# The last product of three chained layers by Strassen's scheme, and halves of a product of two weight matrices added as they are emptied

## The chip, the cores and the metric

The kernel runs on one core of a Trainium2 chip. The metric is device time in microseconds (us); less is better. The time of the kernel before is 646.93 us, the median of three runs (645.35 to 648.14).

## What is computed

The reference chains attention, a gated feed-forward layer and a second block; only the second block is changed.

```python
# x: 896 tokens x 768, from attention (2 batches of 448 tokens, 12 heads) and the gated layer
def _moe2_ref(x, w1, w2, w3, w_out):
    a = x @ w1                 # 896 x 1024
    b = x @ w2                 # 896 x 1024
    h = a * b @ w3             # 1024 x 1024
    return (h @ w_out)         # 1024 x 768
```

The kernel multiplies the two weight matrices first: M = w3 @ w_out (1024 x 768), while it works on earlier stages, and then needs one last product, out = (a * b) @ M. The inputs of the weights come as 64-bit numbers and are turned into 32-bit ones on the core.

## The kernel before

Everything is held transposed: 128 features on the partitions, tokens along the free axis, in two halves `b` of 448 tokens. Every product is taken in three matmuls (`gemm`, lines 791 to 793): each operand is split into a high and a low part of a shorter float format, and high*high, high*low and low*high are added up in one PSUM bank. A split is a copy into the short format (`half`, lines 180 to 184, on ACT, DVE or POOL) and a subtraction on DVE (`rest`, line 187).

The stages that matter here, in order of time, are made from the list `seq` in `experts`:

- "up" and "down" of the gated layer, first half (`h` = 0);
- "prod": the second half of M's inner dimension, eight row blocks `kb` by two column halves of 384, 12 matmuls of 384 columns each. The first half was taken earlier, between the attention's steps, by `last_product`. Both halves of M are emptied from PSUM by `out_`'s `copy` and written to DRAM by its `store` (line 613) as two separate arrays `m32[0]` and `m32[1]`;
- "up" and "down", second half (`h` = 1);
- "two": the products with w1 and w2, for each of eight feature blocks `f` and both token halves 18 matmuls with each matrix. The first result is copied out of its bank (line 839), the second multiplied by it (line 855), and the product `z` is split (`first`, `second`);
- "out": the last product. For each of six output blocks `d` and both token halves, 24 matmuls of 448 columns (eight inner blocks, three matmuls each). Its weights, blocks of M, come back from DRAM through `weights` with kind "sum": two loads of 256 KB (line 255), one addition on DVE (`sum_`, line 259), then a split. The bank is copied out by ACT and stored (line 939).

The order of the instructions on every engine is not written by hand. `Plan` simulates the five engines with a cost for each step, gives every step a rank, and issues on each engine the ready step of lowest rank; the result is a fixed order in which each engine's queue then runs. A step that waits holds up all that stands behind it on its engine. Buffers are rings with a fixed number of turns: `raw` (3) for loaded weights, `hl` (4) for split weights, `sg` (4) for 448-column scratch, `mo` (2) for M's blocks on their way out, and pairs of PSUM banks `m`, `o`, `s` used in turn. The big buffers `A`, `B` (at that time the split input `ys` of "two", one for each token half), `C` (the split w_out of "prod"), `xr0`, `xr1` and `u` have one turn each. SP issues all loads and stores.

Of the kernel before, what the change touches and what calls it, by code (L numbers as in the profile page):

```python
# [38 lines left out]
HJ = CF2 // 2  # L39
NRAW, NHL, EARLY = 3, 4, 4  # L40
# [125 lines left out]
def body(ctx: ExitStack, tc, qk, v, cap, wgv, wdn, rg, w12, w3t, wo2, out):  # L166
# [8 lines left out]
    m32 = dram.tile([2, CF2, P, DM], F32, name="m32")  # L175
# [34 lines left out]
    def layer(es, bounded):  # L210
# [6 lines left out]
        rings |= {n: 1 for n in ("A", "B", "C", "xr0", "xr1", "u")}  # L217
# [20 lines left out]
        def weights(kind, src, n, m, rank, when, get, makes, uses, after=(), ready=()):  # L238

# [8 lines left out]
            def load(e):  # L248
                if kind == "f64":
                    st["t"] = t = ring(wst, "raw", [P, n, m, 2], I32, "wraw")  # L250
                    e.dma_start(out=t, in_=src)
                else:
                    st["t"] = t = ring(wst, "raw", [P, 2, n, m], name="wraw")
                    for i in range(2):
                        e.dma_start(out=t[:, i], in_=src[i])

            def sum_(e):
                st["w"] = st["t"][:, 0]
                e.tensor_tensor(st["w"], st["t"][:, 0], st["t"][:, 1], op=ALU.add)
# [31 lines left out]
            if kind == "f64":  # L291
                a = add(unary, high, rank + 0.1, after=[last], uses=[raw])
                c = add(unary, low, rank + 0.2, after=[last], uses=[raw])
                a = add(("DVE", two), join, rank + 0.3, after=[a, c], uses=[raw])
                last = add(("DVE", two), sign, rank + 0.4, after=[a], uses=[raw])
            else:
                last = add(("DVE", two), sum_, rank + 0.1, after=[last], uses=[raw])
# [289 lines left out]
        def prep_wo(q, rank, when, step):  # L587

            done = wo_done[q] = []

            def get_wo(r):
                def get(new):
                    if q not in wo:
                        wo[q] = ring(big, "BC"[q], [P, 2, HJ, DM], F32R, "wo")
                    return wo[q][:, 0, r : r + 1, :], wo[q][:, 1, r : r + 1, :]

                return get

            for r in range(HJ):
                done.append(  # L600
                    list(weights("f64", wo2[q * HJ + r], 1, DM, rank + (10 * step * r if q else r), when + step * r, get_wo(r), [] if r else [wob[q]], [wob[q]] if r else [],
                                 ready=[done[0][0]] if r else []))
                )

        def out_(q, kb, n, get):
            st = {}

            def copy(e):
                st["o"] = ring(tp, "mo", [P, NH])
                half(st["o"], get()[:, :NH], e)  # L610

            def store(e):
                e.dma_start(out=m32[q, kb][:, n * NH : (n + 1) * NH], in_=st["o"])

            return copy, store

        def last_product():
# [13 lines left out]
            for kb in range(CF2):  # L631
                w3b[kb] = buf("hl")
                w3_done[kb] = list(weights("f64", w3t[0, kb], HJ, P, 1000.5 if kb == 0 else 1003 + kb, 0 if kb == 0 else 3 + kb * 3.5, get_w3(kb), [w3b[kb]], []))

# [14 lines left out]
            for kb in range(CF2):  # L649
                bb = [buf("m") for _ in range(2)]  # L650
                last = {}
                for y in range(2 * HJ):
# [4 lines left out]
                    if r == HJ - 1:  # L657
                        copy, store = out_(0, kb, n, lambda kb=kb, n=n: mb[kb, n])
# [68 lines left out]
        def experts(over, stored):  # L727
# [7 lines left out]
            mv = [m32[q].rearrange("k p c -> p k c") for q in range(2)]  # L735
            seq += [("out", [t[:, i * HJ : (i + 1) * HJ, d * P : (d + 1) * P] for t in mv], HJ, d, i) for d in range(CD) for i in range(2)]
# [13 lines left out]
            def w_of(k):  # L750
                if k not in w_done:
                    what, src, n, _, _ = seq[k]
                    wb[k] = buf("hl")
                    kind, after = ("sum", stored) if what == "out" else ("f64", [])
                    w_done[k] = list(weights(kind, src, n, P, 2000 + 10 * k, 60 + k, get_w(k), [wb[k]], [], after=after))
# [4 lines left out]
            zrb = {b: buf("xr%d" % b) for b in range(B)}  # L760
            u, z, zr, yp, ys, banks, sg = {}, {}, {}, {}, {}, {}, {}
# [6 lines left out]
            n_out = len(seq) - 2 * CD  # L768
            while k < n_out:
                order += [(k, b) for b in range(B)]  # L770
                k += 1
            for d in range(CD):
                order += [(n_out + 2 * d, b) for b in range(B)]
# [4 lines left out]
            def z_at(part, f, b):  # L778
                if f < HF:
                    return u["t"][:, part, f, tok(b)]  # L780
                return zr[b][:, 2 * (f - HF) + part, :]
# [19 lines left out]
            u_done, u_read, y_done, yp_done, y_alloc, yp_alloc, z_done, zr_alloc = {}, {0: [], 1: []}, {}, {}, {}, {}, {}, {}  # L801
            sgb, sg_done = {}, {}
            u_alloc = []
            for s, (k, b) in enumerate(order):
# [6 lines left out]
                half_tiles = [k, k + 1] if what == "out" else [k]  # L811
                a, g = None, 0
                for kk in half_tiles:
                    src, need, held = {
                        "up": (x_at, x_done[b], [xsb[b]]),
                        "down": (u_at, None, [ub]),
                        "prod": (wo_at, None, [wob[1]]),
                        "two": (y_at, y_done.get(b), [yb[b]]),
                        "out": (z_at, None, [ub, zrb[b]]),
                    }[what]  # L820
                    ready = w_of(kk)
                    for c in range(seq[kk][2]):
                        if what == "prod":
                            need = wo_done[1][c]
                        if what == "down":
                            need = u_done[i, b, c]
                        if what == "out":
                            need = z_done[b, g]
                        total = 2 * HJ if what == "out" else n
                        a = add(("PE", 0.53 if what == "prod" else 0.615), gemm(kk, b, c, total, g, src, tag if a is None else None, k), rank + 0.1 * g,  # L830
                                after=[a] + list(need) + ready, makes=[bb] if a is None else [], uses=[wb[kk]] + held + ([bb] if a is not None else []))
                        g += 1
# [17 lines left out]
                elif what in ("up", "two"):  # L850
                    key = (f, b) if what == "up" else ("z", f, b)
                    at = u_at if what == "up" else z_at
# [4 lines left out]
                    def first(e, key=key, f=f, b=b, at=at, what=what):  # L857
                        if what == "up" and "t" not in u:
                            u["t"] = up().tile([P, 2, HF, NT], F32R, tag="u", name="u", bufs=1)
                        if what == "two" and f == HF and b not in zr:  # L860
                            zr[b] = ring(big, "xr%d" % b, [P, 2 * (CF2 - HF), S], F32R, "zr")
                        half(at(0, f, b), sg[key], e)

                    def second(e, key=key, f=f, b=b, at=at):
                        rest(at(1, f, b), sg[key], at(0, f, b), e)
# [3 lines left out]
                    if what == "up":  # L869
                        if not u_alloc:  # L870
                            makes, held, more = [ub], [], list(over)
                        else:
                            more = u_alloc + (u_read[0] if f >= HF else [])
                    elif f >= HF:
                        held = [zrb[b]]
                        if f == HF:
                            makes, held = [zrb[b]], []
                        else:
                            more = zr_alloc[b]
                    else:  # L880
                        more = u_read[0] + u_read[1]
                    i1 = add(("ACT", 0.58), first, late + 0.1, after=[a] + more, makes=makes, uses=[sgb[key]] + held)
                    if what == "up" and not u_alloc:
                        u_alloc.append(i1)
                    if what == "two" and f == HF:
                        zr_alloc[b] = [i1]
                    i2 = add(("DVE", 0.64), second, late + 0.2, after=[i1], uses=[sgb[key], *(makes + held)])
                    if what == "up":
                        u_done[f // HF, b, f % HF] = [i1, i2]
                    else:  # L890
                        z_done[b, f] = [i1, i2]
                elif what == "prod":
                    copy, store = out_(1, f, b, lambda k=k, b=b: banks[k, b])
                    mo = buf("mo")
                    a = add(dict(DVE=0.57, ACT=0.52), copy, late, after=[a], makes=[mo], uses=[bb])
                    stored.append(add(("SP", 0.45), store, -50, after=[a], uses=[mo], size=P * NH * 4))
                elif what == "down":
# [32 lines left out]
                else:  # L930
                    ob = buf("sg")
                    st = {}

                    def copy(e, b=b, k=k, st=st):
                        st["o"] = ring(tp, "sg", [P, S], name="ob")
                        half(st["o"], banks[k, b][:, :S], e)

                    def store(e, d=f, b=b, st=st):
# [74 lines left out]
```

## Time and profile before

| | us |
|---|---|
| median of three runs | 646.93 (645.35 to 648.14) |
| the profiled execution's own time | 644.65 |
| its span, first to last instruction | 642.5 |
| TensorE (PE) busy | 625.0 |
| VectorE (DVE) busy | 390.0 |
| ScalarE (ACT) busy | 277.2 |
| GpSimd (POOL) busy | 162.8 |

The table tells shares of the whole span. What a change in one stage is worth is read from that stage, so the rows below go by stretches of time: "prod" runs from 290.5 to 323.8 us, "two" from 459.7 to 576.7 us, "out" from 576.7 to 636.4 us. Matmuls overlap, so the start of one to the start of the next is the pace, and the duration of one is longer than that.

### The profile page before, as it was taken

Reading aid. Unit: us, or ns where it says so; the run is one execution under the profiler, and the core shown is the slowest. Engines: PE = TensorE matmul, PEld = TensorE weight load, DVE = VectorE, ACT = ScalarE, POOL = GpSimd, SP = SyncE. Lnnn points to the kernel's source line nnn. Section 1 sums busy time; section 2 is a strip of 40 time slices with the busy share of each in tenths; the row PEclk is TensorE's granted clock in tenths of the full one; section 3 lists DMA queues with packets and bytes.
Section 4 is the critical chain, followed back from the end, with each engine's and each line's share of the span. In section 5 each row is a group of like instructions: output and inputs, shape, how many; then the busy total and the mean of one; then the engine's idle time right before and its main releaser. Section 6 shows DMA issues by size and latency. Waiting matters only on the chain.

```text
span 642.5 us, 7766 instructions
## 1 busy us (share of the span) xinstructions
PE 625.0 (97%) x2985; PEld 529.0 (82%) x2985; DVE 390.0 (61%) x474; ACT 277.2 (43%) x383; POOL 162.8 (25%) x161
## 2 busy tenths in 40 slices
PE   6899999999999999999999999999999999999996
PEld 2455556669999999999999999999999999999995
DVE  2898999979867677524765555576565564332300
ACT  6798788965434344223433332233332232121111
POOL 1747532213133344222422222211132221000000
PEclk9899999999999999999999999999999999999999
DMA  8554542325345444225863222333222332224411
GB/s 313 171 201 142 186 142 78 112 73 185 112 153 186 138 141 153 93 71 187 258 211 99 98 99 99 107 129 107 99 99 98 99 118 96 66 65 142 141 46 47
DMA packets 33886, 82.91 MB, mean 129 GB/s; under 512 B 2992, under 2 KB 21040, under 8 KB 33840
## 3 DMA queue, kind: packets, MB, share of 16 engines
q1 hardware_dynamic: 33840, 82.33, 38.4%
q8 instruction: 25, 0.41, 0.3%
q14 instruction: 21, 0.17, 0.1%
HBM read 73.27 MB, written 9.04 MB: 128 GB/s over the span
## 4 chain that ended last, share of the span: by engine, by line
PE 82%; DVE 9%; ACT 5%; issue 2%; POOL 1%; DMA 1%; SPq 0%; ACTq 0%; POOLq 0%; DVEq 0%
PE bank L791 25%; PE bank L793 25%; PE bank L792 25%; PE po L471 3%; DVE sm L499 3%; PE pss L440 2%; ACT t L448 1%; DVE wraw L277 1%; ACT t L454 1%; DVE wraw L281 1%; DVE th L187 1%; PE bank L642 1%; POOL xraw L507 1%; PE bank L644 1%; PE bank L643 1%
## 5 line engine op out<-in xcount | busy, mean ns | idle before, releaser
L273 POOL TENSOR_SCALAR wraw<-wraw 128x768 int32<-128x768 uint32 (+1 forms) x71 | 77.6, 1093 | 195.0 <-DMA wraw<-in_w 85.2
L187 DVE TENSOR_TENSOR whl<-wraw,whl 128x768 fp32r<-128x768 f32 (+1 forms) x80 | 70.1, 876 | 79.5 <-POOL whl L184 65.4
L791 PE MATMUL bank<-xn,whl 128*128 128x448 f32 x288 | 105.6, 367 | 0.5 <-POOL wraw L273 0.5
L792 PE MATMUL bank<-xn,whl 128*128 128x448 f32 x288 | 105.6, 367 | 0.0
L793 PE MATMUL bank<-xn,whl 128*128 128x448 f32 x288 | 105.6, 367 | 0.0
L277 DVE SCALAR_TENSOR_TENSOR wraw<-wraw 128x768 int32<-128x768 int32 (+1 forms) x76 | 70.7, 931 | 48.8 <-POOL wraw L273 43.8
L184 POOL TENSOR_SCALAR whl<-wraw 128x768 fp32r<-128x768 f32 (+1 forms) x47 | 42.4, 902 | 202.0 <-PE bank L793 160.8
L281 DVE SCALAR_TENSOR_TENSOR wraw<-wraw 128x768 int32<-128x768 int32 (+1 forms) x76 | 79.2, 1042 | 1.7
L791 PE MATMUL bank<-u,whl 128*128 128x448 f32 x216 | 79.3, 367 | 0.0
L793 PE MATMUL bank<-u,whl 128*128 128x448 f32 x216 | 79.3, 367 | 0.0
L792 PE MATMUL bank<-u,whl 128*128 128x448 f32 x216 | 79.3, 367 | 0.0
L471 PE MATMUL po<-t,v 128*128 128x448 f32 (+1 forms) x192 | 75.1, 566 | 2.6 <-DVE xraw L182 1.4
L264 ACT ACTIVATE wraw<-wraw 128x768 f32<-128x768 f32 (+1 forms) x59 | 52.1, 882 | 45.8 <-DMA wraw<-in_wgv 16.3
L791 PE MATMUL bank<-y,whl 128*128 128x448 f32 x192 | 70.7, 368 | 0.0
L792 PE MATMUL bank<-y,whl 128*128 128x448 f32 x192 | 70.7, 368 | 0.0
L793 PE MATMUL bank<-y,whl 128*128 128x448 f32 x192 | 70.7, 368 | 0.0
L471 PEld LDWEIGHTS po<-t,v 128*128 128x128 f32 (+1 forms) x192 | 31.5, 192 | 33.5 <-issue 25.4
L791 PEld LDWEIGHTS bank<-xn,whl 128*128 128x128 f32 x288 | 54.1, 188 | 5.7 <-POOL wraw L273 0.8
L793 PEld LDWEIGHTS bank<-xn,whl 128*128 128x128 f32 x288 | 54.1, 188 | 4.9
L792 PEld LDWEIGHTS bank<-xn,whl 128*128 128x128 f32 x288 | 54.1, 188 | 4.7
L180 ACT ACTIVATE whl<-wraw 128x768 fp32r<-128x768 f32 (+1 forms) x33 | 28.3, 858 | 42.2 <-PE bank L793 40.6
L448 ACT ACTIVATE t<-pss,small 128x896 f32<-128x896 f32 x42 | 41.9, 998 | 10.3 <-PE pss L440 8.4
(89 smaller groups left out, 938.8 us busy)
## 6 DMA issues: line engine op xcount, KB each, us to landing
wraw<-in_wgv SPq DMA_DIRECT2D x24, 768.0 KB, 4.4
wraw<-in_w SPq DMA_DIRECT2D x16, 768.0 KB, 4.2
wraw<-in_wdn SPq DMA_DIRECT2D x12, 768.0 KB, 4.2
wraw<-in_w3t SPq DMA_DIRECT2D x16, 512.0 KB, 3.9
wraw<-in_wo SPq DMA_DIRECT2D x8, 768.0 KB, 6.7
m<-mo SPq DMA_DIRECT2D x32, 192.0 KB, 2.7
wraw<-m SPq DMA_DIRECT2D x24, 256.0 KB, 3.2
v<-in_v SPq DMA_DIRECT2D x12, 448.0 KB, 3.8
```

The source lines that it names most:

```text
L180: nc.scalar.activation(out_, in_, AF.Copy)
L184: nc.gpsimd.tensor_scalar(out_, in_, 1.0, 1.0, op0=ALU.mult, op1=ALU.mult)
L187: e.tensor_tensor(lo, raw, r32(hi), op=ALU.subtract)
L264: e.activation(h, h, AF.Copy, scale=2.0**-112)
L273: e.tensor_scalar(l, l.bitcast(U32), 0.876 * 2.0**-29, 0.49, op0=ALU.mult, op1=ALU.add)
L277: e.scalar_tensor_tensor(l, h, 3, l, op0=ALU.logical_shift_left, op1=ALU.bitwise_or)
L281: e.scalar_tensor_tensor(l, h, -(2**31), l, op0=ALU.bitwise_and, op1=ALU.bitwise_or)
L448: e.activation(chunks[g], s[:, :, :S], AF.Tanh, scale=tsc)
L471: e.matmul(pos[2 * p + i][:, :S], vals[p][rows, 6 if c == 3 else 2 * c + i, :], x, start=start, stop=stop)
L791: e.matmul(dst, whi[:, c, :], src(0, g, b), start=(g == 0), stop=False)
L792: e.matmul(dst, whi[:, c, :], src(1, g, b), start=False, stop=False)
L793: e.matmul(dst, wlo[:, c, :], src(0, g, b), start=False, stop=(g == total - 1))
```

## The change

**The last product.** The list `seq` ends with "two"; the stage "out" is replaced by a loop of its own over three pairs `D` of output blocks. M's block pair (two blocks `r` of 128 output features), the inner blocks (even and odd ones) and the token halves make a 2 x 2 by 2 x 2 block product. By Strassen's scheme (Winograd's form) it is taken as seven products for eight; each is four inner blocks `q` by three matmuls of 448 columns. Four sums of blocks of M per `D` (`combine`, S1 to S4) and four differences of blocks of `z` per pair of feature blocks (`less`, the operands 4, 5, 3 and 6) are needed, three more splits of `z` per pair of feature blocks, and additions when the banks are emptied (`plus`): per `D` one copy on ACT and seven additions on DVE for four copies on ACT.

**Homes of z.** The 28 split operands of z lie in `u`, `C`, `xr0`, `xr1` and a new buffer `ux`; a ring `sx` of two holds raw differences.

**Loads of M.** M is stored as one array. Per `D` two loads of 512 KB: the first pair into the ring `raw`, the second and third into `A` and `B`.

**Halves of M.** The first half of M goes to `m32_half`. In "prod" each half block of it (192 KB) is loaded back into an `mo` or `sg` buffer ahead of time, and DVE adds the bank to it on the way out, where DVE or ACT copied the bank before.

The diff, cut to its core:

```diff
-    m32 = dram.tile([2, CF2, P, DM], F32, name="m32")
+    m32 = dram.tile([CF2, P, DM], F32, name="m32")
+    m32_half = dram.tile([CF2, P, DM], F32, name="m32_half")
...
+        rings["sx"] = 2
...
-            mv = [m32[q].rearrange("k p c -> p k c") for q in range(2)]
-            seq += [("out", [t[:, i * HJ : (i + 1) * HJ, d * P : (d + 1) * P] for t in mv], HJ, d, i) for d in range(CD) for i in range(2)]
...
+                    if op == 0:
+                        parts(0, [d], late + 0.1)
+                    elif op == 3:
+                        z_raw[q, 4] = less(4, 3, 0, None, [d, z_raw[q, 0]], late + 0.1)
+                        parts(4, [z_raw[q, 4]], late + 0.2)
+                    elif op == 1:
+                        parts(1, [d], late + 0.1)
+                    else:
+                        t2 = less(5, 2, 4, 4, [d, *z_done[q, 4]], late + 0.1)
+                        parts(5, [t2], late + 0.2)
+                        t3 = less(3, 2, 3, 3, [d, z_raw[q, 4]], late + 0.3)
+                        parts(3, [t3], late + 0.4)
+                        t4 = less(6, 1, 5, 1, [t2, *z_done[q, 1]], late + 0.5)
+                        parts(2, [d], late + 0.6)
+                        parts(6, [t4], late + 0.7)
...
                 elif what == "prod":
-                    copy, store = out_(1, f, b, lambda k=k, b=b: banks[k, b])
-                    mo = buf("mo")
-                    a = add(dict(DVE=0.57, ACT=0.52), copy, late, after=[a], makes=[mo], uses=[bb])
+                    tag = "sg" if (2 * f + b) % 3 else "mo"
+                    load, copy, store = out_(1, f, b, lambda k=k, b=b: banks[k, b], tag)
+                    mo = buf(tag, late)
+                    x = add(("SP", 0.45), load, rank * 0.001 + 60 + k - 1.5, after=halves, makes=[mo], size=P * NH * 4)
+                    a = add(("DVE", 0.57), copy, late, after=[a, x], uses=[mo, bb])
...
+            for D in range(CD // 2):
+                rank, when, late = 6000 + 100 * D, 60 + len(seq) + 2 * D, 900 + 10 * D
+                where = ("raw", "A", "B")[D]
...
+                s1 = combine("S1", "A21", "A22", ALU.add, load, 0)
+                s2 = combine("S2", "S1", "A11", ALU.subtract, [s1], 1)
+                s3 = combine("S3", "A11", "A21", ALU.subtract, [s1], 2)
+                s4 = combine("S4", "A12", "S2", ALU.subtract, [s2], 3)
+                jobs = [("A11", 0, load), ("S1", 4, [s1]), ("A12", 1, load), ("S2", 5, [s2]), ("S3", 3, [s3]), ("S4", 2, [s4]), ("A22", 6, load)]
...
+                for n, (name, op, ready) in enumerate(jobs):
...
+                    i1 = add(dict(POOL=0.75, ACT=0.63), first, i, after=ready, makes=[hb], uses=rawb)
+                    i2 = add(("DVE", 0.7), second, i + 0.5, after=[i1], uses=[hb] + rawb)
...
+                    for q in range(NQ):
+                        a = add(("PE", 0.615), prod(name, op, q, tag), rank + n + 0.1 * q, after=[a] + z_done[q, op] + [i1, i2],
...
+                    if name == "A11":
+                        plus("s1", name, None, [a], late)
+                    elif name == "A12":
+                        done = plus("c11", name, "s1", [a], late), "c11", 0, 0
+                    elif name == "S2":
+                        plus("u2", name, "s1", [a], late + 0.1, at="s1")
+                        plus("u4", "S1", "u2", [ends["S1"]], late + 0.2)
+                    elif name == "S3":
+                        done = plus("c22", name, "u4", [a], late + 0.3), "c22", 1, 1
+                        plus("u3", name, "u2", [a], late + 0.4, at="u2")
+                    elif name == "S4":
+                        done = plus("c12", name, "u4", [a], late + 0.5, at="u4"), "c12", 0, 1
+                    else:
+                        done = plus("c21", name, "u3", [a], late + 0.6, at="u3"), "c21", 1, 0
```

## Rows read from the trace of the kernel before

**Rows 1.** The page: span, and busy time of each engine.
```profile
span 642.5 us, 7766 instructions
PE 625.0 (97%) x2985; PEld 529.0 (82%) x2985; DVE 390.0 (61%) x474; ACT 277.2 (43%) x383; POOL 162.8 (25%) x161
```

**Rows 2.** Waits of PE from 158 us on: total, times, longest.
```profile
PE bank L791 <- POOL wraw L273: 0.5, 1, 0.5
```

**Rows 3.** Busy time by stretch: "prod", second "up"/"down", "two", "out".
```profile
core 0: us, PE busy (x) PEld busy (x) DVE busy (x) ACT busy (x) POOL busy (x), PEclk, DMA share, GB/s
290.80:323.80 33.00, 33.00 (x192) 33.00 (x192) 18.53 (x24) 11.81 (x19) 10.46 (x12) 1.00 0.73 238
323.80:459.70 135.90, 135.90 (x659) 123.46 (x658) 79.90 (x106) 48.29 (x70) 28.34 (x26) 1.00 0.33 113
459.70:576.70 117.00, 117.00 (x567) 106.27 (x567) 58.64 (x74) 31.25 (x48) 19.05 (x18) 1.00 0.29 95
576.70:636.40 59.70, 59.69 (x289) 53.88 (x287) 11.55 (x17) 9.73 (x17) 2.47 (x4) 1.00 0.31 96
```

**Rows 4.** Timeline of "out": first and last matmul, last copy, last store's issue.
```profile
576.71 0.37 PE L791 MATMUL bank<-u,whl 128*128 128x448 f32 x1
...
636.02 0.37 PE L793 MATMUL bank<-zr,whl 128*128 128x448 f32 x1
636.48 0.54 ACT L180 ACTIVATE ob<-bank 128x448 f32<-128x448 f32 x1 [4.41 <-PE bank L793]
637.05 0.33 SPq L939 DMA_DIRECT2D out<-ob  x1
```

**Rows 5.** Timeline of PE: fifteen matmuls in first "up"; begin and end of "prod".
```profile
239.78 0.36 PE L793 MATMUL bank<-xn,whl 128*128 128x448 f32 x1
...
242.82 0.36 PE L793 MATMUL bank<-xn,whl 128*128 128x448 f32 x1
...
290.45 0.34 PE L791 MATMUL bank<-wo,whl 128*128 128x384 f32 x1
...
323.58 0.33 PE L793 MATMUL bank<-wo,whl 128*128 128x384 f32 x1
323.76 0.36 PE L791 MATMUL bank<-xn,whl 128*128 128x448 f32 x1
323.96 0.37 PE L792 MATMUL bank<-xn,whl 128*128 128x448 f32 x1
324.17 0.37 PE L793 MATMUL bank<-xn,whl 128*128 128x448 f32 x1
```

**Rows 6.** Groups by shape on DVE and ACT in "two" and "out": busy, mean ns.
```profile
L855 DVE TENSOR_TENSOR sg<-bank,sg 128x448 f32<-128x448 f32 x15 | 9.4, 624 | 18.5 <-PE bank L793 18.5
L187 DVE TENSOR_TENSOR u<-sg,u 128x448 fp32r<-128x448 f32 x12 | 8.2, 679 | 3.2 <-ACT u L180 3.2
L187 DVE TENSOR_TENSOR zr<-sg,zr 128x448 fp32r<-128x448 f32 x3 | 1.9, 624 | 1.3 <-ACT zr L180 1.3
L180 ACT ACTIVATE zr<-sg 128x448 fp32r<-128x448 f32 x3 | 1.7, 579 | 7.7 <-DVE sg L855 7.7
...
L187 DVE TENSOR_TENSOR whl<-wraw,whl 128x512 fp32r<-128x512 f32 x9 | 6.2, 693 | 17.6 <-ACT whl L180 10.2 <-POOL whl L184 7.3
L259 DVE TENSOR_TENSOR wraw<-wraw 128x512 f32<-128x512 f32 x6 | 4.2, 694 | 12.0 <-DMA wraw<-m 12.0
L180 ACT ACTIVATE whl<-wraw 128x512 fp32r<-128x512 f32 x5 | 3.2, 632 | 10.1 <-PE bank L793 10.1
```

**Rows 7.** Groups by shape over the whole span: further DVE and POOL durations.
```profile
L914 DVE TENSOR_TENSOR yp<-bank,yp 128x448 f32<-128x448 f32 x12 | 7.5, 625 | 12.5 <-PE bank L793 12.5
L182 DVE COPY mo<-bank 128x384 f32<-128x384 f32 x10 | 5.3, 541 | 4.9 <-DMA m<-mo 4.8
L277 DVE SCALAR_TENSOR_TENSOR wraw<-wraw 128x512 int32<-128x512 int32 x16 | 12.1, 756 | 18.6 <-POOL wraw L273 18.6
L184 POOL TENSOR_SCALAR whl<-wraw 128x512 fp32r<-128x512 f32 x22 | 15.9, 724 | 108.5 <-PE bank L793 72.9 <-PE bank L644 16.4 <-issue 14.3
```

**Rows 8.** The page's DMA issues: count, KB each, median us to landing.
```profile
wraw<-in_w3t SPq DMA_DIRECT2D x16, 512.0 KB, 3.9
m<-mo SPq DMA_DIRECT2D x32, 192.0 KB, 2.7
wraw<-m SPq DMA_DIRECT2D x24, 256.0 KB, 3.2
```

**Rows 9.** DMA in "prod", 290.8 to 323.8 us: all, by queue, and stores' landing.
```profile
DMA packets 3021, 7.86 MB, mean 238 GB/s; under 512 B 332, under 2 KB 2104, under 8 KB 3018
q1 hardware_dynamic: 3018, 7.81, 72.9%
m<-mo SPq DMA_DIRECT2D x14, 192.0 KB, 3.4
```

**Rows 10.** Timeline of DVE in "prod": last step of two weight blocks.
```profile
308.67 0.69 DVE L187 TENSOR_TENSOR whl<-wraw,whl 128x512 fp32r<-128x512 f32 x1 [0.54 <-POOL whl L184]
313.19 0.96 DVE L187 TENSOR_TENSOR whl<-wraw,whl 128x768 fp32r<-128x768 f32 x1 [0.77 <-POOL whl L184]
```

**Rows 11.** Waits of SP's queue from 280 us on: total, times, longest.
```profile
SPq L251 <- DVE whl L187: 209.0, 37, 9.4
...
SPq L613 <- ACT mo L180: 12.1, 11, 1.7
SPq L613 <- DVE mo L182: 7.3, 5, 2.6
```

More of the change, by code (lines that the diff above doesn't have):

```diff
@@ L39 @@
 HJ = CF2 // 2
+CS = 7 * CF2 // 2
 NRAW, NHL, EARLY = 3, 4, 4
@@ L248, in load @@
             def load(e):
[L249 to L259, printed above, removed]
+                st["t"] = t = ring(wst, "raw", [P, n, m, 2], I32, "wraw")
+                e.dma_start(out=t, in_=src)
             def high(e):
@@ L753, in w_of @@
                     wb[k] = buf("hl")
-                    kind, after = ("sum", stored) if what == "out" else ("f64", [])
-                    w_done[k] = list(weights(kind, src, n, P, 2000 + 10 * k, 60 + k, get_w(k), [wb[k]], [], after=after))
+                    w_done[k] = list(weights(src, n, P, 2000 + 10 * k, 60 + k, get_w(k), [wb[k]], []))
                 return w_done[k]
@@ L810, in experts @@
                 late = 600 + s
[L811 to L832, printed above, removed]
+                src, need, held = {
+                    "up": (x_at, x_done[b], [xsb[b]]),
+                    "down": (u_at, None, [ub]),
+                    "prod": (wo_at, None, [wob[1]]),
+                    "two": (y_at, y_done.get(b), [yb[b]]),
+                }[what]
+                ready, a = w_of(k), None
+                for c in range(n):
+                    if what == "prod":
+                        need = wo_done[1][c]
+                    if what == "down":
+                        need = u_done[i, b, c]
+                    a = add(("PE", 0.53 if what == "prod" else 0.615), gemm(k, b, c, n, c, src, tag if a is None else None, k), rank + 0.1 * c,
+                            after=[a] + list(need) + ready, makes=[bb] if a is None else [], uses=[wb[k]] + held + ([bb] if a is not None else []))
                 if what == "up" and i == 0:
@@ L880, in experts @@
                     else:
[L881 removed]
+                        more = u_alloc + (u_read[0] if f >= HF else [])
                     i1 = add(("ACT", 0.58), first, late + 0.1, after=[a] + more, makes=makes, uses=[sgb[key]] + held)
[L883 removed]
+                    if not u_alloc:
                         u_alloc.append(i1)
[L885 to L886 removed]
@@ L929, in experts @@
                         y_done[b].append(add(("DVE", 0.64), second, late + 0.2, after=[x], uses=[ypb[b], yb[b]]))
[L930 to L938, printed above, removed]
-                        e.dma_start(out=out[d * P : (d + 1) * P, tok(b)], in_=st["o"])
-                    x = add(("ACT", 0.57), copy, late, after=[a], makes=[ob], uses=[bb])
-                    add(("SP", 0.45), store, -50, after=[x], uses=[ob], size=P * S * 4)
+            mv = m32.rearrange("k p c -> p k c")
```

210 lines of the change are left out of this document (155 added, 55 removed).

## Prediction

> **What bounds the kernel now.** I read the page's busy times first: PE is busy 625.0 of 642.5 us, the next engine 390.0 [rows 1]. A share can hide idle time, so I asked next what PE waits for from 158 us on, when attention is over: one wait of 0.5 us in all [rows 2]. Then the stretches, with the granted clock beside them: in "prod", the second "up"/"down", "two" and "out" PE is busy to the last hundredth, at a granted clock of 1.00, the upper level (2.4 GHz), while DVE has 56%, 59%, 50% and 19% [rows 3]. From 158 us to the end the time is thus the number of matmuls times their pace. A matmul taken out of these stages is worth its pace, as long as nothing else comes late for PE.
>
> The pace is read from starts. "Out" is 288 matmuls (6 blocks x 2 token halves x 24); from the first start to the last are 287 steps in 636.02 - 576.71 = 59.31 us, or 0.2067 us each [rows 4]. This pace is not the only one the trace shows: in the first "up" fifteen matmuls of the same size take 242.82 - 239.78 = 3.04 us, 0.2027 each. The step up comes with the second 448-column matmul after "prod" (324.17 - 323.96 = 0.21) and stays to the end [rows 5]. The granted clock reads 1.00 on both sides [rows 3], so no change of the clock's level explains it. I don't know what sets it; it comes back as a rival.
>
> **The change part by part.** *Matmuls.* 3 pairs `D` x 7 products x 4 inner blocks x 3 = 252 for 288, of the same 448 columns. 36 fewer x 0.2067 = 7.44 us off, all of it on the path. The ends of this price are the two paces, 7.30 and 7.44; I take the one of this stage.
>
> The Trainium skill (TensorE: Matmul & The Clock Gate, Back-to-back issue gap) gives N / 2.4 + 2.5 ns for an isolated gap, an estimate of 189 ns for 448 columns, by which the 36 would give 6.8 us. The trace disagrees at 206.7 ns [rows 4], and the sum goes by the trace.
>
> *The differences and splits of z, in "two".* Per pair of feature blocks 4 subtractions and 3 further splits: on DVE 4 + 3 steps, on ACT 3. A subtraction of two scratch buffers has no row; the nearest reads the same two operands' worth from SBUF at 448 columns, 0.624 to 0.679 us [rows 6], and I take 0.65. Four pairs: 28 x 0.65 = 18.2 us on DVE, 12 x 0.58 = 7.0 on ACT. DVE goes from 58.6 to some 77 of 117 us, ACT from 31.3 to 38 [rows 3]: beside PE's work, and free as long as the last results come in time.
>
> *That end of "two".* It is where the change adds a dependency. Before, "out" began with blocks finished long ago and reached the last one after 21 matmuls, 4.3 us later. Now the fourth product (S2, with operand 5) needs the difference made from the very last bank. The cover is the three products before it, 36 x 0.2067 = 7.44 us. The chain is product out of the bank 0.62, difference 0.65, ACT half 0.58, rest 0.62 [rows 6], with some 0.1 us between steps about 2.9 us: covered, with 4.5 us over. If DVE takes all eight late z steps in an unlucky order, 8 x 0.64 + 0.58 = 5.7 us, still covered. Only if the preparation of the first `D` (4 sums and 7 rests, 11 x 0.69 = 7.6 us) stood ahead as well would it take 13.3 and stall PE for 5.9 us. Those ranks are behind z's, and the weights' buffers are free far earlier, so I take 0 and keep 0 to 5.9 as the bound.
>
> *The sums of M's blocks and their splits.* Per `D` 4 sums, 7 rests and 7 emptying additions on DVE: 4 x 0.694 + 7 x 0.693 + 7 x 0.625 (an addition of a bank to an SBUF buffer, line 914) = 12.0 us [rows 6, 7]. The sums read every second block of 128; no row reads so, the nearest are the contiguous sum, 0.694, and a step that reads every second word, 0.756 [rows 6, 7], which adds 0.2 us at most. One `D` lasts 84 x 0.2067 = 17.4 us on PE, so DVE is 69% busy where it was 19%. It is not the bound, and a product's split weights (four turns of `hl`) can be made up to three products, 7.4 us, ahead, for half and rest of 1.3 us. Cost 0. What goes: twelve sums, twelve splits and the copies on ACT, all hidden before.
>
> *Loads of M.* The first pair goes through `raw`, free once the last weights of "two" are split. The second waits for buffer `A`, read until the last matmul of token half 0, 18 matmuls before the end of "two": 576.7 - 3.7 = 573.0 us. Two loads of 512 KB, one behind the other; no row has 512 KB from M, the nearest are 512 KB of weights in 3.9 us and 256 KB from M in 3.2 [rows 8], so 7.8 to 12.8 us for both: landed by 580.8 to 585.8, and wanted by 576.7 + 17.4 = 594.1 less 1.3 for the split. At least 7 us over. The third (`B`) has 17 us more. Behind a waiting load on SP stand stores, for which nobody waits but a scratch buffer's next turn. Cost 0.
>
> *"Prod" with the first half added.* All 16 emptyings move to DVE (11 of them waited for ACT before, 5 for DVE [rows 11]): 11 x some 0.56 = 6.2 us, DVE 18.5 to 24.7 of 33 us [rows 3, 7]. Each now also waits for a load of 192 KB, issued by SP; queued behind a waiting addition on DVE are the weights' steps, and PE waits for those. Cushion: the last weight block of "prod" is finished at 309.4 and used at 290.45 + 7 x 4.16 = 319.6 (a block takes (323.76 - 290.45) / 8 = 4.16); the first one of "up" is finished at 314.2 for 323.8 [rows 5, 10]. So 9 to 10 us. Six buffers take turns, so one comes round every 12.5 us, of which the addition takes 0.6 and the store 3.4 [rows 9], which leaves 8 us for a load of about the store's length. The first six loads can be issued in "down", when `sg` is idle. DMA: ten more loads, 2 MB onto 7.86 MB, 73% to some 91% busy [rows 9]. Tight but no overflow. Cost 0; the bound is in rival C.
>
> *The tail.* After the last matmul comes an addition on DVE (0.625) for a copy on ACT (0.54) [rows 4, 7]: +0.08 us. Store and end as before.
>
> **The sum.** Span 642.5 - 7.44 + 0.08 = 635.1 us. The profiled execution's own time is 2.15 us above its span: 637.3. The median of the runs shown, 646.93, lies 2.28 us above the profiled execution, and I count from it: 646.93 - 7.36 = **639.6 us**.
>
> **The rivals.** *A, the pace.* If PE comes out of "prod" at 0.2027 (its waits there change), 1224 matmuls of the second "up", "down" and "two" and 252 of the last stage gain 0.004 us each, 5.9 us: 633.7. For it: the trace shows both paces of one shape. Against it: PE's own instructions up to the end of "two" stay the same. The other way, the slow pace from the first "up" on, 656 matmuls x 0.004 = 2.6 us: 642.2. *B, DVE comes last.* The stall at the end of "two" (0 to 5.9) or smaller ones at each `D`: 640 to 645.5. For it: 69% on DVE, in a fixed order made from planned costs. Against: 4.5 us or more over at every place costed above. *C, slower.* In "prod" SP stands in front of weight loads that wait for a buffer, up to 9.4 us at a time [rows 11]. If the loads of M's first half queue behind such waits, DVE waits for the load, the weights' last step waits behind it on DVE, and that step is what frees the next weight buffer: a load's landing is then paid in line, twice for each row block: 2 x (3.4 + 0.6 + 0.5) = 9 us for PE's 4.16 [rows 9], 8 x 4.9 = 39 us, less the cushions of 10 and 12.5: +16.5 us, 656. It decides once DVE is over 10 us late. Against it: six buffers and 8 us for each load. *D, it does not do what it says*, that is 252 matmuls but as much idle as was saved, 646.9: it would need 7.4 us of B.
>
> **How the numbers follow.** Forecast 0.74; A fast 0.10, A slow 0.03; B with D 0.09; C 0.04. 0.5% of 646.93 is 3.2 us, about what a measurement can tell from no change, so faster means under 643.7: 0.74 + 0.13 and a third of B, 0.90. The same: the rest of B, 0.06. Slower: C, 0.04. The range goes from rival A's fast end, rounded down, to its slow end and the cheaper half of B: 633.0 to 643.0.
>
> **What would show it.** In the profile after: 252 matmuls in some 52.1 us after "two", each 12 of a product in 2.48 us; PE without waits over 0.5 us from 158 us on; DVE some 77 us busy in "two" and 12 per `D`. The waits of PE name the step that failed: DVE rest or difference right after "two" (B), the same at 17.4 us steps (loads or sums), weights right after "prod" (C). The start-to-start pace in the second "up" tells A. Wrong outright if PE waits over 4 us in all.

## The result, and the profile after

The changed kernel takes 637.33 us, the median of four runs (636.01 to 638.36), beside 646.14 us for four runs of the kernel before: a ratio of 0.986, 95% interval 0.982 to 0.990. A second comparison on one chip gave 636.42 us (six runs) beside 645.41 us (eleven runs), ratio 0.9855 (0.9831 to 0.9879). The ratios leave out runs over 1.5% above the fastest of the same kernel, which bears on one run of 642.5 us in each of two kernels of the experiments. The forecast was 639.6 us, within 633.0 to 643.0: it was right, the gain somewhat larger than the 7.36 us forecast. The section on the reasons tells how much of the rest is accounted for.

The page of the changed kernel, profiled execution of 638.36 us (span and busy time, to be read against [rows 1]):

```profile
span 636.6 us, 7787 instructions
PE 619.9 (97%) x2949; PEld 522.0 (82%) x2949; DVE 427.2 (67%) x543; ACT 284.4 (45%) x392; POOL 158.0 (25%) x153
```

36 matmuls fewer, 5.1 us less of PE, and 37 us more of DVE. PE's waits from 150 us on have no row at all in this trace, where the kernel before had one [rows 2]. The stretches of time in the changed kernel ("prod", second "up"/"down", "two", the last product; columns as in [rows 3]):

```profile
292.16:325.45 33.29, 33.29 (x194) 33.28 (x192) 22.19 (x34) 10.58 (x14) 6.03 (x7) 1.00 0.84 278
325.45:459.36 133.91, 133.91 (x649) 121.66 (x649) 81.44 (x106) 46.35 (x67) 28.12 (x26) 1.00 0.35 119
459.36:578.40 119.04, 119.04 (x577) 108.15 (x576) 68.32 (x96) 37.76 (x59) 18.65 (x18) 1.00 0.25 80
578.40:630.65 52.25, 52.24 (x253) 47.12 (x251) 33.67 (x54) 14.33 (x24) 0.84 (x1) 1.00 0.26 80
```

The last product fell from 59.7 to 52.2 us; PE is idle for no more than 0.01 us of any stretch, and DVE in the last one rose from 11.6 to 33.7 us. The chain that ended last in that stretch is PE alone until its last matmul, then one step of DVE:

```profile
578.56 52.09 PE bank L1031 x252
...
630.68 0.62 DVE sg L1043
```

### The profile page after: what moved, and what is told of

It reads as the page before. It is cut to its first block, busy times and chain, and to the rows that moved or that the text cites. A ratio compares the mean times of both kernels' runs of the same rounds, so it can differ in the third digit from the quotient of the medians.

```text
span 636.6 us, 7787 instructions
## 1 busy us (share of the span) xinstructions
PE 619.9 (97%) x2949; PEld 522.0 (82%) x2949; DVE 427.2 (67%) x543; ACT 284.4 (45%) x392; POOL 158.0 (25%) x153
## 4 chain that ended last, share of the span: by engine, by line
PE 84%; DVE 7%; ACT 5%; issue 2%; POOL 1%; DMA 1%; SPq 0%; DVEq 0%; POOLq 0%
PE bank L808 22%; PE bank L809 22%; PE bank L807 22%; PE bank L1031 8%; PE po L461 4%; ACT t L438 2%; DVE sm L489 2%; PE pss L430 2%; ACT t L444 2%; PE bank L640 1%; PE bank L641 1%; PE bank L642 1%; DVE wraw L270 1%; DVE wraw L274 1%; POOL xraw L497 1%
## 5 line engine op out<-in xcount | busy, mean ns | idle before, releaser
L189 DVE TENSOR_TENSOR whl<-wraw,whl 128x768 fp32r<-128x768 f32 (+1 forms) x86 | 75.7, 882 | 70.4 <-POOL whl L186 58.2
L266 POOL TENSOR_SCALAR wraw<-wraw 128x768 int32<-128x768 uint32 (+1 forms) x67 | 76.1, 1135 | 170.8 <-DMA wraw<-in_w 57.8
L270 DVE SCALAR_TENSOR_TENSOR wraw<-wraw 128x768 int32<-128x768 int32 (+1 forms) x76 | 71.4, 939 | 40.8 <-POOL wraw L266 33.6
L274 DVE SCALAR_TENSOR_TENSOR wraw<-wraw 128x768 int32<-128x768 int32 (+1 forms) x76 | 76.8, 1011 | 1.5
L186 POOL TENSOR_SCALAR whl<-wraw 128x768 fp32r<-128x768 f32 (+1 forms) x38 | 34.0, 895 | 166.8 <-PE bank L809 125.2
L182 ACT ACTIVATE whl<-wraw 128x768 fp32r<-128x768 f32 (+1 forms) x48 | 38.1, 795 | 70.6 <-PE bank L809 31.5
L257 ACT ACTIVATE wraw<-wraw 128x768 f32<-128x768 f32 (+1 forms) x55 | 48.5, 882 | 39.4 <-DMA wraw<-in_wgv 14.3
L809 PE MATMUL bank<-u,whl 128*128 128x448 f32 x144 | 53.0, 368 | 0.0
L807 PE MATMUL bank<-u,whl 128*128 128x448 f32 x144 | 53.0, 368 | 0.0
L808 PE MATMUL bank<-u,whl 128*128 128x448 f32 x144 | 53.0, 368 | 0.0
```

Of the source, the lines that this page charges most:

```text
L182: nc.scalar.activation(out_, in_, AF.Copy)
L189: e.tensor_tensor(lo, raw, r32(hi), op=ALU.subtract)
L257: e.activation(h, h, AF.Copy, scale=2.0**-112)
L266: e.tensor_scalar(l, l.bitcast(U32), 0.876 * 2.0**-29, 0.49, op0=ALU.mult, op1=ALU.add)
L270: e.scalar_tensor_tensor(l, h, 3, l, op0=ALU.logical_shift_left, op1=ALU.bitwise_or)
L274: e.scalar_tensor_tensor(l, h, -(2**31), l, op0=ALU.bitwise_and, op1=ALU.bitwise_or)
```

## The experiments

**The second part alone.** Which of the two parts gives the gain? The kernel before, with M's halves added on the way out and the last product left at eight products:

```diff
-    m32 = dram.tile([2, CF2, P, DM], F32, name="m32")
+    m32 = dram.tile([CF2, P, DM], F32, name="m32")
+    m32_half = dram.tile([CF2, P, DM], F32, name="m32_half")
...
-                last = add(("DVE", two), sum_, rank + 0.1, after=[last], uses=[raw])
...
-                    a = add(dict(DVE=0.57, ACT=0.52), copy, late, after=[a], makes=[mo], uses=[bb])
+                    a = add(("DVE", 0.57), copy, late, after=[a, x], uses=[mo, bb])
```

> The kernel before with the second part of the change alone: the halves of M are added as the second one's banks are emptied, M is stored once, the last product keeps its eight products (288 matmuls) and loads M without the sum on DVE. Theory (every step of this part is hidden behind the matmuls, so the gain is all Strassen's): the time of the kernel before within 0.5%, no wait of PE over 0.5 us, last stage 59.5 us. Rival (the part costs, since all 16 emptyings wait for a load on DVE): 1 to 16 us slower, with waits of PE for weights right after 'prod'. Second rival (it gives part of the gain, by taking 12 sums and half of the loads away at the end): 1 to 3 us faster with a shorter last stage.

Ratio to the kernel before 0.9994 (0.9975 to 1.0012), ten runs beside nineteen. "Prod" and the last product, and all waits of PE from 150 us on:

```profile
293.37:326.65 33.28, 33.28 (x193) 33.28 (x192) 22.42 (x32) 10.61 (x14) 5.54 (x7) 1.00 0.82 275
579.50:639.20 59.70, 59.70 (x290) 53.96 (x288) 7.39 (x11) 9.73 (x17) 2.47 (x4) 1.00 0.21 70
...
PE bank L795 <- ACT mo L181: 0.9, 1, 0.9
```

The one wait lies before the first "up", not behind "prod". The part is worth nothing and costs nothing that the runs can tell (0.25% at most): all of it is hidden, the removed 12 sums too. So the gain has to be Strassen's, which the next run tests.

**288 matmuls again.** Is it the count? The changed kernel with one product of each `D` taken twice:

```diff
-                    for q in range(NQ):
+                    for t in range(2 * NQ if name == "A12" else NQ):
+                        q = t % NQ
```

> The changed kernel with one product of each D taken twice into the same bank, so 288 matmuls in the last stage again; all else of Strassen's scheme stays. Theory (the gain is the number of matmuls times their pace): 36 x 0.2067 = 7.44 us above the changed kernel, the last stage 59.5 us, about the time of the kernel before. Rival (part of the gain is from the shorter loads, the sums or the order of the end): less than 5 us above the changed kernel.

Ratio to the kernel before 1.0005 (0.9984 to 1.0026). The last product of this kernel, its first and last matmuls, and those of the changed kernel:

```profile
580.63:640.50 59.87, 59.87 (x290) 54.06 (x288) 33.73 (x54) 14.33 (x24) 0.84 (x1) 1.00 0.22 70
...
580.84 0.57 PE L1031 MATMUL bank<-z,whl 128*128 128x448 f32 x2
...
639.74 0.78 PE L1031 MATMUL bank<-z,whl 128*128 128x448 f32 x3
```

```profile
578.40 0.78 PE L1031 MATMUL bank<-z,whl 128*128 128x448 f32 x3
...
629.86 0.78 PE L1031 MATMUL bank<-z,whl 128*128 128x448 f32 x3
```

DVE has the 33.7 us of the changed kernel, PE the 59.7 us of the one before, and the time is that of the one before. Sums, loads and the new order are worth nothing that the runs can tell (0.3% at most); the 36 matmuls are worth the gain. The exact 7.44 us is met by the stage: from the start of its first matmul to that of the third from the end it takes 639.74 - 580.84 = 58.90 us, in the changed kernel 629.86 - 578.40 = 51.46, which is 7.44 less. The medians of the two kernels, from two comparisons, lie 8.7 us apart; the part on the reasons takes that up.

**No cover for the last operand.** What does the cover at the end of "two" hide? S2 is moved ahead of the other products of the first `D`, its block that comes last ahead of its others:

```diff
+                if D == 0:
+                    jobs.insert(0, jobs.pop(3))
...
+                        q = NQ - 1 - at if name == "S2" and D == 0 else at
+                        a = add(("PE", 0.615), prod(name, op, q, tag, at=at), rank + n + 0.1 * at, after=[a, prev] + z_done[q, op] + [i1, i2],
```

> The changed kernel with the first D's products in another order: the one that needs operand 5 (S2) is first, its last inner block, made from the last bank of 'two', first of all. Nothing covers the chain then. Theory (the cover of three products hides the chain of product out of the bank 0.62, difference 0.65, half 0.58, rest 0.62 and the steps between): PE waits 2.9 to 3.3 us once, right after 'two', last stage 55 to 55.5 us for 52.1. Rival (DVE's queue at that point holds other work, so the chain is longer than costed): 5 to 6 us. What the pace does after such a wait is seen too: 0.2067 us if the pace is kept, 0.2027 if a wait of PE resets it (then 1.0 us of the wait comes back).

(In this order one partial sum of the first `D` is overwritten before its last use, so one output block does not hold its product; the steps and their sizes are the same.) PE's waits from 570 us on, and three stretches: from the end of "two" to the first matmul, the next 4 us, the rest:

```profile
PE bank L1034 <- ACT z L182: 2.0, 1, 2.0
PE bank L1034 <- DVE z L189: 0.5, 1, 0.5
...
576.06:578.20 2.14, 0.16 (x2) 0.01 (x1) 1.92 (x4) 1.84 (x4) 0.00 (x0) 1.00 0.26 49
578.20:582.20 4.00, 3.47 (x9) 2.88 (x10) 3.15 (x6) 1.01 (x2) 0.00 (x0) 0.57 1.19 308
582.20:631.50 49.30, 49.30 (x244) 45.46 (x243) 28.65 (x45) 11.53 (x19) 0.62 (x1) 1.00 0.17 58
```

The stage takes 55.4 us for the 52.2. The chain of four steps takes some 3 us until the rest is there, as costed, and it is fully covered in the changed kernel. PE's waits are 2.5 us in two parts, not 2.9 to 3.3 in one. Not in the expectation: after PE had stood still, the granted clock went to the lower level for a while (0.57 on average over the next 4 us), which cost over 1 us (an estimate: six matmuls at 0.373 us for 0.207, and a part of three more). The rest of the stage then ran at the faster pace (49.30 us for 243 matmuls, 0.203 each), and that gave about 1 us back. That the length of the stage falls within the expected 55 to 55.5 us is thus partly luck: the two nearly cancel.

**How much room DVE has.** The rest of each weight split in the last stage is taken twice, then three times:

```diff
-                        rest(st["w", name][1], block(name), st["w", name][0], e)
+                        for _ in range(2):
+                            rest(st["w", name][1], block(name), st["w", name][0], e)
```

> The changed kernel with the rest of each of the 21 weight splits of the last stage taken twice (the same result written again): 7 x 0.69 = 4.8 us more DVE work per D, 12.0 + 4.8 = 16.9 us for the 17.4 us that PE needs per D. Theory (DVE has the room that was costed): PE waits under 1 us in all, last stage 52.1 to 53 us. Rival B (the end hangs on DVE, and only just not): PE waits of 2 us or more per D, 6 us or more in all.

> The same with each rest taken three times: 9.7 us more per D, 21.7 us of DVE work for 17.4 us on PE. Theory (DVE's work, by its sum, is the next bound): 3 x 21.7 + 5.1 for z = 70 us, of which some 11 us of the first D's weights can be done before 'two' ends, so the last stage takes about 59 us, 7 us more, and PE waits for DVE at each product of the second and third D. Rival (the fixed order hides it, or the loads are the next bound): under 2 us more.

PE's waits from 570 us on, first with two rests, then with three, and the last stage of each:

```profile
PE bank L1031 <- DVE whl L189: 1.6, 1, 1.6
...
580.00:633.40 53.40, 51.77 (x253) 47.06 (x251) 45.40 (x72) 13.20 (x22) 2.05 (x3) 1.00 0.25 78
```

```profile
PE bank L1031 <- DVE whl L189: 7.9, 3, 3.8
...
579.21:641.20 61.99, 54.07 (x253) 48.20 (x251) 57.68 (x90) 12.04 (x20) 3.72 (x5) 0.97 0.22 67
```

Three rests cost 9.7 us, somewhat more than the 7 expected. PE waited 7.9 us in three places, not at each product; about 1.5 us more is the clock, which fell to its lower level after the longest of the waits and stayed there for nine matmuls of 0.373 us:

```profile
601.51 0.47 PE L1031 MATMUL bank<-z,whl 128*128 128x448 f32 x1 [2.95 <-DVE whl L189]
...
622.57 0.47 PE L1031 MATMUL bank<-z,whl 128*128 128x448 f32 x1 [3.77 <-DVE whl L189]
...
624.10:627.50 3.40, 3.40 (x11) 2.99 (x11) 3.33 (x5) 0.55 (x1) 0.80 (x1) 0.50 0.02 7
```

DVE, busy for 57.7 of the 62.0 us, is the next bound. Two rests cost one wait of 1.6 us and a stage 1.2 us longer, more than "under 1 us in all" and less than rival B's 6: the sum (16.9 of 17.4 us) left room on average, but not at the first product of the second `D`, whose split weights came late. The same place in the changed kernel itself, DVE's steps ahead of that product, which begins 84 matmuls after 578.40, at 595.8 us:

```profile
589.72 1.28 DVE L1012 TENSOR_TENSOR wraw<-wraw 128x512 f32<-128x512 f32 x2
591.00 1.16 DVE L1043 TENSOR_TENSOR sg<-bank,sg 128x448 f32<-128x448 f32 x2
592.08 1.29 DVE L189 TENSOR_TENSOR whl<-wraw,whl 128x512 fp32r<-128x512 f32 x2
```

The first of the two rests at 592.08 ends about 592.7: 3 us before its use. The 7 us over that the prediction had for this place were those of the loads; the sums of M (line 1012) and the additions stand between the landing and the rest.

**Two buffers for the loads in "prod".** Was rival C's loop real?

```diff
-                    tag = "sg" if (2 * f + b) % 3 else "mo"
+                    tag = "mo"
```

> The changed kernel with the loads of M's first half in 'prod' all going through the two 'mo' buffers, none through 'sg': a buffer comes round every 4.2 us instead of 12.5. Theory (rival C's mechanism is real, and it is the six buffers that keep it out): load some 3.5, addition 0.6 and store some 3 us in line make 7 us or more for each pair of products that PE does in 4.2, so 'prod' takes some 55 us for 33; less the cushion of six banks and of the weights, 10 to 25 us slower than the changed kernel, with PE waits for DVE inside 'prod'. Rival (the loads were never near mattering): under 2 us slower.

653.4 us, 15 to 17 above the changed kernel. PE's waits from 285 us on, and "prod" up to the first matmul of "up":

```profile
PE bank L807 <- DVE mo L605: 9.9, 3, 4.0
...
290.67:338.59 47.92, 38.02 (x194) 37.15 (x192) 26.71 (x38) 13.71 (x17) 7.63 (x9) 0.89 0.63 204
```

47.9 us for 33.3, with waits for banks that DVE had not emptied: 14.6 us, within the 10 to 25 expected. Part of it is the clock again (granted 0.89 on average, after PE had stood still). The mechanism is real, and what keeps it out of the changed kernel is the six buffers.

**The pace after a wait.** In the profile of the changed kernel the first "up" ran at 0.2067 us, in that of the kernel before at 0.2027 [rows 5]. Its start follows the 384-column matmuls without a gap:

```profile
158.08 0.33 PE L642 MATMUL bank<-wo,whl 128*128 128x384 f32 x1
158.25 0.36 PE L807 MATMUL bank<-xn,whl 128*128 128x448 f32 x1
158.45 0.37 PE L808 MATMUL bank<-xn,whl 128*128 128x448 f32 x1
158.66 0.37 PE L809 MATMUL bank<-xn,whl 128*128 128x448 f32 x1
158.86 0.37 PE L807 MATMUL bank<-xn,whl 128*128 128x448 f32 x1
```

0.20 and then 0.21, as after "prod" in [rows 5]; in the kernel before this start came after PE had waited 0.5 us [rows 2]. So a wait was put in at the end of "prod": the first matmul of the second "up" takes the bank that the last product of "prod" has filled.

```diff
+                    if skip:
+                        bank(first)
...
+                if what == "up" and i == 0 and b == 0 and f == HF:
+                    if f:
+                        tag = ("m", "o", "s")[(turn - 2) // 2 % 3]
+                        turn -= 1
+                    skip, hold = buf(tag), None
```

> The changed kernel with one wait of PE put in: the first matmul of the second 'up' writes the bank that the last product of 'prod' has just filled, so it waits for DVE to empty it. Theory P (the pace of the 448-column matmuls is set at their start: 0.2027 us when they begin after PE stood still, 0.2067 when they follow the 384-column ones without a gap): one wait of 0.7 to 2 us at the end of 'prod', then 0.2027 us to the end, 1476 x 0.004 = 5.9 us back, so 4 to 5 us faster than the changed kernel in its slow-paced profile (span some 632 us). Rival (the pace changes by itself, or by the time since the start): 0.7 to 2 us slower than the changed kernel, pace 0.2067.

Span 632.3 us in the profile. The end of "prod" in it, and matmuls further on:

```profile
325.66 0.34 PE L811 MATMUL bank<-wo,whl 128*128 128x384 f32 x1
327.01 0.44 PE L809 MATMUL bank<-xn,whl 128*128 128x448 f32 x1 [1.02 <-DVE mo L605]
327.29 0.37 PE L810 MATMUL bank<-xn,whl 128*128 128x448 f32 x1
327.49 0.36 PE L811 MATMUL bank<-xn,whl 128*128 128x448 f32 x1
...
330.53 0.36 PE L811 MATMUL bank<-xn,whl 128*128 128x448 f32 x1
```

From 327.49 to 330.53, fifteen matmuls, it is 3.04 us: 0.2027 us, and so to the end of this profile. One profile is one draw, so the kernel was run again beside the changed one, and a second wait put ahead of the first "up" too.

> The changed kernel as it is, beside the kernel before on one chip, for the ratio with more runs. Theory (36 matmuls of 0.2067 us and nothing else; the pace is drawn for each stage anew, for both kernels alike): 7.3 to 7.5 us below the kernel before on average, ratio 0.988 to 0.989, and single runs spread over some 5 us in both. Rival (the 8.8 us of the first comparison are the change's own): ratio under 0.987.

> The kernel with the wait at the end of 'prod' again, timed beside the changed kernel. Theory (after a wait of PE the pace is 0.2027 in a good half of the cases, after the 384-column stream without a gap always 0.2067): the runs fall in two groups some 6 us apart, the lower one near 630 to 634, the upper one 1 us above the changed kernel's; on average 1 to 3 us faster than the changed kernel. Rival (the one profile was chance of another kind): 1 us slower on average, one group.

> The same with a second wait ahead of the first 'up', where the trace of the changed kernel shows its matmuls following the 384-column ones without a gap. Theory: the first 'up' and 'down' too are drawn after a wait, 656 x 0.004 = 2.6 us in a good half of the runs for some 0.4 us more of waiting: on average about 1 us faster than with one wait. Rival: no faster than with one.

| | median us | all runs | ratio to the kernel before |
|---|---|---|---|
| changed kernel, second comparison | 636.42 | 635.8 to 636.7 (6) | 0.9855 (0.9831 to 0.9879) |
| one wait, beside the first experiments | 636.40 | 634.1 to 640.0 (4) | 0.9892 (0.9849 to 0.9934) |
| one wait, second comparison | 635.10 | 632.5 to 642.5 (6) | 0.9824 (0.9790 to 0.9859) |
| two waits, second comparison | 638.78 | 632.2 to 642.5 (6) | 0.9861 (0.9816 to 0.9906) |

The intervals overlap, so the wait can't be called a better version. The expected two groups of runs, 6 us apart, are not there, and the second wait did not make the kernel faster than the first. The runs with a wait spread over 10 us where the changed kernel's beside them stay within 1 us. The paces explain only a part of that: 0.2067 throughout with a wait of 1.7 us would give some 640 us (an estimate: span 636.6, the wait, and 1.8 outside the span), not the 642.5 of the slowest runs, of which there are no traces. In the profiles, the second "up" ran at 0.2027 after the wait in both of the kernel with one wait, and at 0.2067 in the one with two. In the run with two buffers for the loads it came after a wait too; there the clock fell to its lower level after three matmuls, and at the upper level again the pace was 0.2067. Without a wait there it ran at 0.2067 in all eight profiles in which it follows "prod" without a gap, of the kernels before and after and of six further runs. The first "up" came after a gap in ten profiles and ran at 0.2027 in five of them; twice it followed without a gap and began at 0.2067, and in one of these two (the run with the last operand first) it went over to 0.2027 after 18 matmuls, with no wait in the trace. Theory P's "always fast after a wait" is wrong. That a wait redraws the pace fits nearly all that was seen, but that one change shows that a wait is not the only thing that does, and why one or the other is drawn no run shows.

## Why the prediction was right, step by step

*The matmuls.* 252 in 52.09 us by the chain, 0.2067 each, as forecast. The experiment with 288 shows that nothing else in the change gives a gain beyond its interval of 0.3%.

*The Trainium skill's gap* (TensorE: Matmul & The Clock Gate, Back-to-back issue gap), an estimate of 189 ns for 448 columns, stays too low: the runs show 202.7 or 206.7 ns.

*The gain's size.* Forecast 7.36 us, measured 8.8 and 9.0 by the medians. The interval of the first comparison (6.3 to 11.4 us) holds the forecast, that of the second (7.8 to 10.9) just does not, so the expectation of a ratio of 0.988 to 0.989 there was missed and its rival, under 0.987, was met. The term that was off is the one carried over as a constant, all that lies ahead of the first "up", its pace, and what follows the last matmul. Two profiles with the same paces (first "up" at 0.2027, the rest at 0.2067), of the kernel before (span 642.5) and the changed kernel in the second comparison (span 634.6), differ by 7.9 us: 7.44 for the matmuls, 0.2 for an earlier start of "up" (158.83 for 159.05 us), and 0.3 after the last matmul. The two starts:

```profile
159.05 0.44 PE L791 MATMUL bank<-xn,whl 128*128 128x448 f32 x1 [0.49 <-POOL wraw L273]
```

```profile
158.83 0.44 PE L807 MATMUL bank<-xn,whl 128*128 128x448 f32 x1 [0.18 <-ACT mo L182]
```

Outside the span, 0.4 us more went (644.65 - 642.5 = 2.15 before, 638.36 - 636.6 = 1.76 after), and the experiment with the second part alone has this too (647.02 - 645.2 = 1.82). That makes 8.3 us at equal paces. For the remaining 0.5 to 0.7 us there is an argument only: the six runs of the changed kernel lie within 0.94 us of each other, and the profiled one of them had the faster pace in its first "up"; the kernel before spread from 643.2 to 648.0 beside them. If fewer of its runs drew the faster pace there, which is worth 648 x 0.004 = 2.6 us (the prediction counts 656 matmuls there, the trace has 648), its median is higher for that reason and not for the change. It fits that the kernel before had a median of 644.09 us in 19 runs beside the first experiments, on the same chip; from there to the 636.42 it is 7.7 us. Traces of those runs were not kept, so this stays open.

*Rival A* was half right. The pace did not change at the end of "prod" by itself, but it differs between executions of one kernel at the first "up": 0.2067 in the first profile of the changed kernel, 0.2027 in the second. The prediction's slow side of 2.6 us is what the first shows: span 636.6 for the 634.6 of the second, less 0.6 for an earlier start.

*The differences and splits of z.* The steps that had no row before, in the changed kernel (subtractions of z in "two", sums of M in the last stage):

```profile
L883 DVE TENSOR_TENSOR sx<-sg,sx 128x448 f32<-128x448 f32 x6 | 3.8, 681 | 0.1
...
L883 DVE TENSOR_TENSOR sg<-sg,sx 128x448 f32<-128x448 f32 x3 | 1.8, 616 | 0.0
...
L1012 DVE TENSOR_TENSOR wraw<-wraw 128x512 f32<-128x512 f32 x8 | 5.2, 684 | 0.0
```

A subtraction took 0.616 to 0.681 us, for 0.65. DVE in "two" rose from 58.6 to 68.3 us, not to 77. Six of the 28 new steps ran only after the stretch (below: three subtractions, and four rests where the kernel before had one), which is 3.7 us; the rests of z took 0.62 us where twelve of them had taken 0.68 [rows 6]; and the sums and splits of M within the stretch, left out of the prediction's sum, came to 4.9 us after 6.2. Together that is some 6 of the 8.7 us. The chain at the end of "two" was costed at 2.9 us and took some 3; the last bank's steps in the changed kernel:

```profile
578.60 0.62 DVE L868 TENSOR_TENSOR sg<-bank,sg 128x448 f32<-128x448 f32 x1 [1.75 <-PE bank L809]
579.26 1.17 DVE L883 TENSOR_TENSOR sx<-sg,sx 128x448 f32<-128x448 f32 x2
580.34 0.62 DVE L883 TENSOR_TENSOR sg<-sg,sx 128x448 f32<-128x448 f32 x1
580.88 1.57 DVE L189 TENSOR_TENSOR z<-sx,z 128x448 fp32r<-128x448 f32 x2
582.37 1.15 DVE L189 TENSOR_TENSOR z<-sg,z 128x448 fp32r<-128x448 f32 x2
```

S2's rest, the first of the two at 580.88, ends about 581.7, 3 us after the last bank, and the block is read 45 matmuls after 578.40, at 587.7. The cover was 9.3 us, not 7.44, since S2 reads three finished blocks first.

*The sums and splits of M.* DVE was busy for 33.7 us in the last stage. By groups of steps, 30.2 us are the last product's own (costed at three times 12.0, less the 4.9 done ahead in "two") and 5.1 the late steps of z; they overlap a little. The sums that read every second block took 0.684 us for the 0.694 of contiguous ones [rows 6]. The step "7 us over" for the second `D` was wrong: 3 us, as the run with two rests shows. Rival B was nearer than its 0.09 looked: 4.8 us more DVE work per `D` did bring a wait of 1.6 us.

*"Prod".* DVE 18.5 to 22.2 us (24.7 costed), DMA busy 83.4% of the stretch (91% costed). The loads took 5.5 us to land there where some 3.4 were costed, the stores 5.8, the weights 6.9 for 4.8, all in a busier DMA [rows 9]. Weights in "prod" of the kernel before:

```profile
wraw<-in_wgv SPq DMA_DIRECT2D x6, 768.0 KB, 4.8
```

In the changed kernel, DMA in that stretch, DVE's wait for the loads, and the last step of the first weight block of "up":

```profile
q1 hardware_dynamic: 4148, 9.22, 83.4%
...
wraw<-in_wgv SPq DMA_DIRECT2D x5, 768.0 KB, 6.9
m<-mo SPq DMA_DIRECT2D x14, 192.0 KB, 5.8
mo<-m_half SPq DMA_DIRECT2D x10, 192.0 KB, 5.5
...
DVE mo L605 <- DMA mo<-m_half: 1.2, 2, 0.7
...
315.72 0.95 DVE L189 TENSOR_TENSOR whl<-wraw,whl 128x768 fp32r<-128x768 f32 x1
```

DVE waited 1.2 us for loads in all. The first weight block of "up" was finished at 316.7 for 325.45 us, 8.8 us ahead, where the kernel before had 9.6 [rows 10]. Rival C's 9.4 us at a time is SP's longest wait for a buffer from 280 us on [rows 11]; within "prod" it was 6.9 us.

*The tail.* An addition of 0.62 on DVE for a copy of 0.54, as forecast. The 0.08 can't be seen in the time: from the start of the last matmul to the end of the span it is 6.48 us before, 6.28 and 6.20 in the two profiles of the changed kernel, and 6.30 with the second part alone, which keeps the copy.

## What to carry to other kernels

When PE never waits, an edit is worth the matmuls it removes times their pace in that stage, and the rest of the work is to show that everything added has a cover: find, at each new dependency, the first matmul that reads the late result, and count DVE's own queue between the load and that matmul, not the load alone. A margin by sums (69% busy) says little about the tightest place: double the suspected work once and see where PE begins to wait. Before reading 1 us into a comparison, look at the start-to-start pace of the unchanged stages in both traces.

## What the runs showed of the hardware

Matmuls of one shape, back to back and at a granted clock of 1.00 (2.4 GHz), have two paces, 0.2027 and 0.2067 us for 448 columns. One is kept for hundreds of matmuls, mostly until PE next waits or the shape changes, and after the 384-column matmuls without a gap it began at 0.2067 in every profile here (ten starts). What sets it stays open. Runs of one kernel beside each other lay up to 5 us apart (643.2 to 648.0), and the pace of the first "up" and "down" alone accounts for 2.6 us of such a spread. The start of the first "up" varies as well: 158.55 and 159.96 us in the two profiles of the kernel with one wait.

The granted clock fell to its lower level (1.2 GHz) for some matmuls after a wait of PE of 2.0 us and one matmul at the end of "two", after one of 3.8 us and seven matmuls in the run with three rests, and around waits of up to 4.0 us in the one with two buffers. Single waits of 0.9 to 1.6 us elsewhere left it at 1.00, and so did one of 2.95 us in the run with three rests: here the clock did not go by the length of the wait alone.
